# Attention and GEGLU block: a wait each for the two kinds of score products, a later tanh, and a rebuilt end

## The chip, the cores and the metric

The kernel runs on one core of a Trainium2 chip. The metric is device time in microseconds (us). The kernel before takes 1311.1 us, the median of three runs (1309.63 to 1311.43). A core has five engines that work beside each other, each with its own queue in order: TensorE (PE in the profile, with its weight loads listed as PEld), VectorE (DVE), ScalarE (ACT), GpSimd (POOL) and SyncE (SP), which here issues the transfers. They wait for each other through semaphores.

## What is computed

One transformer block on x of 1 x 2048 x 512 in bf16, cut to what matters:

```python
h  = x + A(layernorm(x))                 # 32 heads of 16
h2 = h + B(layernorm(h))                 # GEGLU, 512 -> 1792 -> 512
# A: q, k, v = split(xn @ wqkv); p = softmax(q @ k.T * 16**-0.5); (p @ v) @ wo
# B: (gelu_tanh(hn @ w_gate) * (hn @ w_up)) @ w_down
```

The softmax takes off the maximum of each row before the exponential, so the scores are made twice: once with queries on the partitions, to find the maximum, and once with keys on the partitions, to be exponentiated and multiplied with V.

## The kernel before

**Units and ticks.** The work is cut into 64 units: eight groups `gi` of 256 query rows, eight slots of four heads each. A unit has 16 ticks, and the main loop at the end of the kernel emits the work of all engines tick by tick. In a tick there are two streams. The first makes the maxima: `p1_pair` issues two matmuls of 32 x 512 (L665) into two banks of `pbank` (a bank is 128 x 512 in float32; there are eight), and `p1_consume` lets DVE reduce both banks with one maximum (L674). It has banks 0 to 3, two pairs in turn. The second stream runs `P2_START` = 24 ticks behind: `p2_tile` is called twice, each call two matmuls of 32 x 256 (L735) into one bank, and `p2_consume` lets ACT exponentiate each bank (L747) into one of 34 tiles named PTM, PTE and PTG. It takes its banks from a list of four (4 to 7), shared with the dense work. So the first stream alone runs in ticks 0 to 23, both in 24 to 1023, and the second alone in ticks 1024 to 1047, which is called the drain here.

**Maxima.** POOL joins the maxima in three steps (L685 to L692 and L700 to L708), a transfer transposes them, and POOL adds them into QT (L719).

**Dense work.** Everything else of TensorE is cut into pieces by Python generators and one piece (or a few, ahead of the second stream) is issued per tick by `dense.piece()`: the projections of q, k and v; `item_pv`, the product with V (L761, 16 matmuls a piece, four pieces a unit, with a fixed place in the unit); `item_ofin`, which transposes the result and normalises it (POOL: L796 takes the power -1 of 16 columns, L800 multiplies); `item_oproj`; and the feed-forward network, `item_gate` and `item_up` (L948) for seven pairs of columns f of each group, and `item_down` (L996). A piece states a cost of up to 3. Where a tick's piece costs under 2, `dummy` fills up with matmuls of 128 x 512 on ones (L1150), whose result nobody reads.

**GELU beside attention.** A gate tile is copied by ACT to `g_sb`. `gelu_chain` puts three operations into POOL's stream (L938, L939, L940), and when the last of them is emitted, `later` is deferred by one tick and then emits the tanh on ACT (L931); it waits further where ACT has other additional work in this tick or the one before (`act_extra`). One tick later `second` adds two more POOL operations (L936, L937), and a last one multiplies with the up tile into GUT (L989). There are two buffers for a chain, taken by f modulo 2; `item_gate` waits while its buffer is busy. `PoolStream` gives POOL a budget of 1.19 us a tick, from costs that are written in by hand, and issues in order.

**Waits.** `Plan.op` works out which semaphores an instruction must wait for. Between `group_begin` and `group_end` all waits of the instructions are taken together and put in front of the first one:

```python
            P.group_begin("pe")
            t1 = p1_pair(tick // 16, tick % 16, gp1) if p1_ok else []
            t2l = [p2_tile(t2 // 16, t2 % 16, 1 - gp1, 0)] if p2_ok else []
            P.group_end("pe")
```

So the pair for the maximum and the first of the two exponential tiles start when both DVE has left the pair's banks and ACT has left the tile's bank. The second tile has its own wait.

**The end.** After the drain, `tail_b` finishes the last group alone: the last slot's result is normalised (`tail_norm`, `tail_onT`), the last quarter of the output projection is added (L1108), the second layer norm is done for its two row tiles, the result is transposed (`tail_hnT`), and gate, up and down products of group 7 follow. `fill(n)` issues dense pieces that are left (the down products of group 6, L996, closed by the residual in L1000), or dummies, up to a cost of n. The norm before: for tile 1 ACT copies with a running sum (L1111) and squares with a running sum (L1113), and POOL works out mean, variance, power -0.5 and the normalised tile (`ln2_from_sums`, `ln2_finish`: L892 to L895, L910 to L913); for tile 0 DVE copies and takes statistics (L1115 to L1117), and POOL does the rest (`ln2_tail`, L902, and `ln2_finish` again), behind tile 1.

Of the kernel before, what the change touches and what calls it, by code (L numbers as in the profile page):

```python
# [209 lines left out]
ACT = mybir.ActivationFunctionType  # L210
ALU = mybir.AluOpType
# [5 lines left out]
EPS = 1e-5  # L217
# [5 lines left out]
ADDX = 4  # L223
LAGX = 8
PAUSE = 1


def bass_sequential_preLN__mha_block__geglu_ffn__prompt_kernel(nc, A_x, A_wqkv, A_wo, B_x, B_w_gate, B_w_up, B_w_down, out):
    dbg = None
    with ExitStack() as es:  # L230
# [236 lines left out]
        def defer(k, fn):  # L467
            deferred.append((dense.now + k, fn))
# [426 lines left out]
            o(lambda e: e.tensor_tensor(out=rstd2[:, tt_], in0=rstd2[:, tt_], in1=htmp[:, tt_], op=ALU.subtract), reads=[("rstd2", t), ("htmp", t)], writes=[("rstd2", t)])  # L895
            return ops + ln2_finish(gi, k, t)

        def ln2_tail(gi, k, t):
            tt_ = slice(t, t + 1)
            ops = []  # L900
            o = lambda fn, reads, writes, cost=0.2: ops.append((cost, lambda: P.op("pool", fn, reads=reads, writes=writes)))
            o(lambda e: e.tensor_scalar(out=rstd2[:, tt_], in0=mv2[:, t, 1:2], scalar1=EPS, scalar2=None, op0=ALU.add), reads=[("mv2", t)], writes=[("rstd2", t)])  # L902
            return ops + ln2_finish(gi, k, t)

        def ln2_finish(gi, k, t):
            hh = g_h(gi, k)
            tt_ = slice(t, t + 1)
# [13 lines left out]
        def gelu_chain(par, dE):  # L921

            th_ready[par] = False
            gs, ts_ = g_sb[:, par, :], th_sb[:, par, :]
            o = lambda cost, fn, reads, extra=(): (cost, lambda: P.op("pool", fn, reads=reads, writes=[("th", par)], extra_deps=extra))
            def later(n):
                if not force[0] and (dense.now in act_extra or (n < 3 and (dense.now - 1) in act_extra)):
                    defer(1, lambda: later(n + 1))
                    return
                act_extra.add(dense.now)  # L930
                P.op("act", lambda e: e.activation(out=ts_, in_=ts_, func=ACT.Tanh, scale=GC), reads=[("th", par)], writes=[("th", par)])  # L931
                defer(1, second)
            def second():
                def done():
                    th_ready[par] = True
                pool.add([o(0.62, lambda e: e.tensor_scalar(out=ts_, in0=ts_, scalar1=1.0, scalar2=0.5, op0=ALU.add, op1=ALU.mult), [("th", par)]),  # L936
                          o(1.27, lambda e: e.tensor_tensor(out=ts_, in0=ts_, in1=gs, op=ALU.mult), [("th", par), ("g", par)])], then=done)  # L937
            pool.add([o(1.04, lambda e: e.tensor_tensor(out=ts_, in0=gs, in1=gs, op=ALU.mult), [("g", par)], dE),  # L938
                      o(0.62, lambda e: e.tensor_scalar(out=ts_, in0=ts_, scalar1=0.044715, scalar2=1.0, op0=ALU.mult, op1=ALU.add), [("th", par)]),  # L939
                      o(1.27, lambda e: e.tensor_tensor(out=ts_, in0=ts_, in1=gs, op=ALU.mult), [("th", par), ("g", par)])], then=lambda: defer(1, lambda: later(0)))  # L940

        def gate_up_mms(b, gi, f, w, nm):
            hT = hnT_l[gi % 2]
# [154 lines left out]
        def tail_b():  # L1098
            P.op("act", lambda e: e.activation(out=htmp[:, 0:1], in_=nhalf[:, 0:1], func=ACT.Gelu_apprx_tanh), reads=["nhalf"], writes=[("htmp", 0)])
            fill(2)  # L1100
            while not a_done[0]:
                fill(1)
            in_bank(tail_norm)
            fill(2)
            in_bank(tail_onT)
            fill(2)
            for k in range(2):
                P.op("pe", lambda e, k=k: e.matmul(pbank[:, k, :], OnT[:, k, 3, :], wo_sb[:, 3, :], start=False, stop=True),  # L1108
                     reads=[("OHb", 0), "wo"], writes=[("pb", k)], sig=True)
            t0 = 2 * GL  # L1110
            P.op("act", lambda e: e.activation(out=g_h(GL, 1), in_=pbank[:, 1, :], func=ACT.Copy, accum_out=hsum[:, t0 + 1:t0 + 2]),  # L1111
                 reads=[("pb", 1)], writes=[("h", 1, 1), ("hsum", t0 + 1)])
            P.op("act", lambda e: e.activation(out=hn_sb[:, 1, :], in_=g_h(GL, 1), func=ACT.Square, accum_out=hsq[:, t0 + 1:t0 + 2]),  # L1113
                 reads=[("h", 1, 1)], writes=[("OH", 1), ("hsq", t0 + 1)])
            P.op("dve", lambda e: e.tensor_copy(out=g_h(GL, 0), in_=pbank[:, 0, :]), reads=[("pb", 0)], writes=[("h", 1, 0)])  # L1115
            P.op("dve", lambda e: e.bn_stats(out=stats2[:, t0, :], in_=g_h(GL, 0)), reads=[("h", 1, 0)], writes=[("stats2", t0)])
            P.op("dve", lambda e: e.bn_aggr(out=mv2[:, t0, :], in_=stats2[:, t0, :]), reads=[("stats2", t0)], writes=[("mv2", t0)])  # L1117
            pool.add(ln2_from_sums(GL, 1, t0 + 1))
            pool.add(ln2_tail(GL, 0, t0))
            fill(14)  # L1120
            for k in (1, 0):
                in_bank(tail_hnT, k)
            fill(2)
            while dense.busy():
                dense.pause = 0
                dense.piece()
                run_deferred(tick, flush=True)
            gb = [2, 3, 4, 5, 6, 7]
            NP = NFC // 2
            for f in range(NP + 2):  # L1130
                if f < NP:
                    for it, b in ((item_gate, gb[(2 * f) % 6]), (item_up, gb[(2 * f + 1) % 6])):
                        for _ in it(b, GL, f):
                            pass
                if f >= 2:
                    for fc in (2 * (f - 2), 2 * (f - 2) + 1):
                        for k in range(2):
                            down_mm(k, GL, k, fc)
            dG = rdeps("G", [("x", cc) for cc in range(NCH)])
            for k in range(2):  # L1140
                down_last(k, GL, k)
                if k == 0:
                    P.op("act", lambda e: e.activation(out=out_sb[:, 0, :], in_=pbank[:, 0, :], func=ACT.Copy), reads=[("pb", 0)], writes=[("osb", 0)], extra_deps=dG)
                else:
                    P.op("dve", lambda e: e.tensor_copy(out=out_sb[:, 1, :], in_=pbank[:, 1, :]), reads=[("pb", 1)], writes=[("osb", 1)], extra_deps=dG)
                P.dma("sp", lambda e, k=k: e.dma_start(out=outv[:, 2 * GL + k, :], in_=out_sb[:, k, :]), ("out", k), reads=[("osb", k)], writes=[("outd", 2 * GL + k)])

        def dummy(b, n):
            for i in range(n):
                P.op("pe", lambda e: e.matmul(pbank[:, b, :], ident[:], ones_bf[:, 0:512], start=True, stop=True),  # L1150
                     reads=["ident", "ones_bf"], writes=[("pb", b)], sig=False)
# [4 lines left out]
        while True:  # L1156
            p1_ok = tick < 16 * NU
            t2 = tick - P2_START
            p2_ok = (0 <= t2 < 16 * NU)
            if not p1_ok and not p2_ok:  # L1160
                break
            if tick == P2_START - 4:
                dense.single = True
                if dense.gen is not None:
                    banks.free.remove(dense.bank)
            if p2_ok and not p2_started:
                p2_started = True
            dve_free[0] = not p1_ok
            dense.tick(tick)
            gp1 = tick % 2  # L1170
            P.group_begin("pe")
            t1 = p1_pair(tick // 16, tick % 16, gp1) if p1_ok else []
            t2l = [p2_tile(t2 // 16, t2 % 16, 1 - gp1, 0)] if p2_ok else []
            P.group_end("pe")
            if p2_ok:
                t2l.append(p2_tile(t2 // 16, t2 % 16, 1 - gp1, 1))
            if t1:
                p1_consume(tick // 16, t1)
                if tick % 16 in (8, 12):
                    pool.spend(0.7)  # L1180
                    negm_part(tick // 16, 1 if tick % 16 == 8 else 2)
                if tick % 16 == 15:
                    pool.spend(1.8)
                    negm_pre(tick // 16)
                    negm_post(tick // 16)
            if t2l:
                p2_consume(t2 // 16, t2l)
            if p2_ok and t2 % 16 == 0:
                dense.add(item_pv, t2 // 16, front=True, est=5, not_before=tick + PV_T[0])
            cost = dense.piece()  # L1190
            if cost and not p2_started:
                dense.piece()
            if (cost or 0) < 2:
                dummy(banks.free[0], 2 - (cost or 0))
            run_deferred(tick)
            pool.tick()
            if w_pieces and tick % 16 in (7, 9, 11, 13):
                w_piece()
            tick += 1
# [39 lines left out]
```

## Time and profile before

| what | value |
|---|---|
| median of three runs | 1311.1 us (1309.63 to 1311.43) |
| the profiled execution | 1310.51 us, of which the span of instructions is 1308.4 us |
| mean granted clock of TensorE | 0.986 |
| PE, DVE, ACT, POOL busy | 1179.9, 1203.9, 1201.2, 763.6 us |
| 1024 reductions for the maximum (L674, DVE) | 1173.8 us, from 35.1 to 1236.2 us |
| 2048 exponentials (L747, ACT) | 735.5 + 226.1 + 135.8 us |
| fillers (L1150, PE) | 822, 258.2 us |
| tanh (L931, ACT) | 49, 30.9 us; ACT waited 11.4 us for them |
| DVE waiting for score products in front of a maximum | 39.4 us in all |
| drain and end, 1235 to 1308.4 us | 73.4 us; granted clock 0.66 and 0.91 in its two halves |

The page gives the busy time of each engine and then its groups of instructions: line, engine, operation, what is written and read, the count, the busy time and the mean time of one, and behind a bar the idle time of the engine just ahead of them with what ended most of it. A line of the timeline has the start, the length, engine, line, operation and, in brackets, the idle time ahead and its releaser. Busy times of ACT and DVE overlap a little from one instruction to the next: an exponential is listed at 643 ns, and four in a row take 1.96 us. A releaser is inferred: a wait that is put down to ACT may also have been the queue itself.

### The profile page before, as it was taken

Reading aid. Unit: us, or ns where it says so; the run is one execution under the profiler, and the core shown is the slowest. Engines: PE = TensorE matmul, PEld = TensorE weight load, DVE = VectorE, ACT = ScalarE, POOL = GpSimd, SP = SyncE. Lnnn points to the kernel's source line nnn. Section 1 sums busy time; section 2 is a strip of 40 time slices with the busy share of each in tenths; the row PEclk is TensorE's granted clock in tenths of the full one; section 3 lists DMA queues with packets and bytes.
Section 4 is the critical chain, followed back from the end, with each engine's and each line's share of the span. In section 5 each row is a group of like instructions: output and inputs, shape, how many; then the busy total and the mean of one; then the engine's idle time right before and its main releaser. Section 6 shows DMA issues by size and latency. Waiting matters only on the chain.

```text
span 1308.4 us, 31442 instructions
## 1 busy us (share of the span) xinstructions
PE 1179.9 (90%) x12678; PEld 408.4 (31%) x12678; DVE 1203.9 (92%) x1101; ACT 1201.2 (92%) x2440; POOL 763.6 (58%) x1534
## 2 busy tenths in 40 slices
PE   4999988999998999999999999999999999989998
PEld 2222222333223332233223332233323332233325
DVE  5899999999999999999999999999999999999702
ACT  3599999999999999999999999999999999999962
POOL 5567663477536773477635774467734775367721
PEclk9999999999999999999999999999999999999959
DMA  3110003200010000100011000100001000100000
GB/s 129 45 29 25 16 24 126 73 5 6 5 28 14 6 5 8 34 6 6 4 29 14 6 4 10 30 9 4 6 26 17 4 6 5 28 14 6 14 1 17
DMA packets 48689, 27.45 MB, mean 21 GB/s; under 512 B 34977, under 2 KB 47009, under 8 KB 48545
## 3 DMA queue, kind: packets, MB, share of 16 engines
q1 hardware_dynamic: 48544, 25.44, 7.4%
q8 instruction: 101, 1.65, 0.5%
q14 instruction: 44, 0.35, 0.1%
HBM read 11.80 MB, written 2.10 MB: 11 GB/s over the span
## 4 chain that ended last, share of the span: by engine, by line
ACT 29%; PE 29%; DVE 24%; POOL 14%; issue 3%; DMA 1%; POOLq 0%
DVE PM L674 23%; ACT PTM L747 15%; PE pbank L761 6%; ACT PTG L747 5%; PE pbank L665 5%; PE pbank L1150 5%; PE pbank L735 5%; POOL LINV L796 4%; PE pbank L996 4%; ACT PTE L747 3%; ACT th_sb L931 2%; POOL th_sb L940 2%; POOL th_sb L938 2%; PE pbank L615 1%; PE pbank L563 1%
## 5 line engine op out<-in xcount | busy, mean ns | idle before, releaser
L674 DVE TENSOR_REDUCE PM<-pbank 128x2 f32<-128x1024 f32 x1024 | 1173.8, 1217 | 39.4 <-PE pbank L735 21.0
L747 ACT ACTIVATE PTM<-pbank 128x512 bf16<-128x512 f32 x1388 | 735.5, 643 | 20.2 <-PE pbank L735 12.0
L735 PE MATMUL pbank<-QT,KT 32*128 32x256 bf16 x4096 | 490.3, 275 | 19.2 <-ACT PTM L747 10.0
L665 PE MATMUL pbank<-KT,QT 32*128 32x512 bf16 x2048 | 398.4, 385 | 12.0 <-DVE PM L674 5.4
L1150 PE MATMUL pbank<-ones_bf,ident 128*128 128x512 bf16 x822 | 258.2, 390 | 37.2 <-ACT u_sb L528 8.3
L747 ACT ACTIVATE PTG<-pbank 128x512 bf16<-128x512 f32 x420 | 226.1, 632 | 5.0 <-PE pbank L735 3.4
L665 PEld LDWEIGHTS pbank<-KT,QT 32*128 32x128 bf16 x2048 | 99.0, 91 | 352.6 <-DVE PM L674 148.8
L735 PEld LDWEIGHTS pbank<-QT,KT 32*128 32x128 bf16 x4096 | 160.9, 92 | 72.0 <-ACT PTM L747 34.9
L761 PE MATMUL pbank<-PTM,VA 128*17 128x256 bf16 x2776 | 157.1, 279 | 14.8 <-PE pbank L761 0.2
L747 ACT ACTIVATE PTE<-pbank 128x512 bf16<-128x512 f32 x240 | 135.8, 643 | 3.8 <-PE pbank L735 2.2
L700 POOL TENSOR_TENSOR MX<-PM,MX 128x8 f32<-128x8 f32 x64 | 12.9, 202 | 168.2 <-DVE PM L674 168.2
L796 POOL TENSOR_TENSOR LINV<-OAT,negone 128x16 f32<-128x16 f32 (+1 forms) x32 | 92.7, 2898 | 12.8 <-DVE OAT L517 12.8
L1150 PEld LDWEIGHTS pbank<-ones_bf,ident 128*128 128x128 bf16 x822 | 49.6, 97 | 146.1 <-ACT PTM L747 88.7
L689 POOL TENSOR_TENSOR MX<-PM,MX 128x8 f32<-128x8 f32 x64 | 13.0, 203 | 119.2 <-DVE PM L674 119.2
L761 PEld LDWEIGHTS pbank<-PTM,VA 128*17 128x17 bf16 x2776 | 42.7, 87 | 108.9 <-PE pbank L761 77.0
L948 PE MATMUL pbank<-hnT_l,wg_sb 128*128 128x256 bf16 x448 | 67.9, 277 | 4.2 <-ACT PTG L747 0.6
L948 PE MATMUL pbank<-hnT_l,wu_sb 128*128 128x256 bf16 x448 | 67.4, 276 | 3.2 <-ACT PTG L747 0.2
L996 PE MATMUL pbank<-wd_sb,GUT 128*128 128x512 bf16 x224 | 61.5, 386 | 3.6
L940 POOL TENSOR_TENSOR th_sb<-th_sb,g_sb 128x512 f32<-128x512 f32 x49 | 62.2, 1269 | 4.1
L937 POOL TENSOR_TENSOR th_sb<-th_sb,g_sb 128x512 f32<-128x512 f32 x49 | 62.1, 1267 | 2.9
L989 POOL TENSOR_TENSOR GUT<-th_sb,u_sb 128x512 bf16<-128x512 f32 x49 | 62.2, 1269 | 2.7
L719 POOL TENSOR_TENSOR QT<-QT,STG 128x256 bf16<-128x256 bf16 x64 | 42.8, 669 | 33.9 <-DMA STG<-ST 33.9
(128 smaller groups left out, 1074.6 us busy)
## 6 DMA issues: line engine op xcount, KB each, us to landing
QKS<-QKS SPq DMA_DIRECT2D x32, 112.0 KB, 2.1
x_sb<-in_A_x_dram SPq DMA_DIRECT2D x4, 512.0 KB, 5.4
xres<-in_A_x_dram SPq DMA_DIRECT2D x16, 128.0 KB, 2.2
out_dram<-out_sb SPq DMA_DIRECT2D x16, 128.0 KB, 1.7
wg_sb<-in_B_w_gate_dram SPq DMA_DIRECT2D x4, 448.0 KB, 4.8
wu_sb<-in_B_w_up_dram SPq DMA_DIRECT2D x4, 448.0 KB, 4.8
wqkv_sb<-in_A_wqkv_dram SPq DMA_DIRECT2D x1, 1536.0 KB, 10.2
wd_sb<-in_B_w_down_dram SPq DMA_DIRECT2D x3, 512.0 KB, 5.9
```

What stands on the lines that cost most here:

```text
L665: P.op("pe", lambda e, g=g, b=b: e.matmul(pbank[:, b, :], QT[32 * g:32 * g + 32, c, slot, 128 * qt:128 * qt + 128], KT[32 * g:32 * g + 32, ...
L674: P.op("dve", lambda e: e.tensor_reduce(out=PM[:, par, qt, kc, g:g + 2], in_=pbank[:, b:b + 2, :], axis=AX.X, op=ALU.max), reads=[("pb", b ...
L735: P.op("pe", lambda e, kt=kt, i=i: e.matmul(pbank[:, b, 256 * i:256 * i + 256], KT[32 * g:32 * g + 32, slot, 128 * kt:128 * kt + 128], QT[ ...
L747: P.op("act", lambda e, b=b, pi=pi: e.activation(out=PTt(pi), in_=pbank[:, b, :], func=ACT.Exp), reads=[("pb", b)], writes=[("PT", pi)], e ...
L761: P.op("pe", lambda e, g=g, kt=kt, pi=pi, i=i: e.matmul(pbank[32 * g:32 * g + 17, b, 0:256], VA[:, kt, 4 * slot + g, :], PTt(pi)[:, 256 * ...
L796: P.op("pool", lambda e: e.tensor_tensor(out=li, in0=oat4[:, :, :, 16], in1=negone[:, 0:8 * ns].rearrange("p (q h) -> p q h", q=2), op=ALU ...
L937: o(1.27, lambda e: e.tensor_tensor(out=ts_, in0=ts_, in1=gs, op=ALU.mult), [("th", par), ("g", par)])], then=done)
L940: o(1.27, lambda e: e.tensor_tensor(out=ts_, in0=ts_, in1=gs, op=ALU.mult), [("th", par), ("g", par)])], then=lambda: defer(1, lambda: lat ...
L948: P.op("pe", lambda e, dc=dc, fc=fc, i=i: e.matmul(pbank[:, b, 256 * i:256 * i + 256], w[:, dc, 128 * fc:128 * fc + 128], hT[:, dc, :], st ...
L989: P.op("pool", lambda e: e.tensor_tensor(out=o_ap, in0=shp(ts_), in1=shp(us), op=ALU.mult), reads=[("th", par), ("u", par)], writes=o_keys ...
L996: P.op("pe", lambda e: e.matmul(pbank[:, b, :], GUT[:, fc, 128 * k:128 * k + 128], wd_sb[:, fc, :], start=(fc == 0), stop=False), reads=[( ...
L1150: P.op("pe", lambda e: e.matmul(pbank[:, b, :], ident[:], ones_bf[:, 0:512], start=True, stop=True), reads=["ident", "ones_bf"], writes=[( ...
```

## The change

Four edits. The group around the score products is taken away, so each instruction has its own wait. The tanh is deferred by two ticks in place of one. In the drain a tick is filled up to a cost of 3 in place of 2. The second layer norm of the end is written anew: statistics for both tiles on DVE, copies on ACT, two POOL operations for both tiles together, normalising on DVE; the filler behind it has cost 18 in place of 14, and the tiles are transposed in the order 0, 1.

```diff
+TANH_LAG = 2
...
-                      ...], then=lambda: defer(1, lambda: later(0)))
+                      ...], then=lambda: defer(TANH_LAG, lambda: later(0)))
...
             t0 = 2 * GL
-            P.op("act", ... activation(out=g_h(GL, 1), in_=pbank[:, 1, :], func=ACT.Copy, accum_out=hsum[...]))
-            P.op("act", ... activation(out=hn_sb[:, 1, :], in_=g_h(GL, 1), func=ACT.Square, accum_out=hsq[...]))
-            P.op("dve", ... tensor_copy(out=g_h(GL, 0), in_=pbank[:, 0, :]))
-            P.op("dve", ... bn_stats(out=stats2[:, t0, :], in_=g_h(GL, 0)))
-            P.op("dve", ... bn_aggr(out=mv2[:, t0, :], in_=stats2[:, t0, :]))
-            pool.add(ln2_from_sums(GL, 1, t0 + 1))
-            pool.add(ln2_tail(GL, 0, t0))
-            fill(14)
-            for k in (1, 0):
+            tok = P.op("dve", ... bn_stats(out=stats2[:, t0, :], in_=pbank[:, 0, :]))
+            P.op("act", ... activation(out=g_h(GL, 1), in_=pbank[:, 1, :], func=ACT.Copy))
+            P.op("act", ... activation(out=g_h(GL, 0), in_=pbank[:, 0, :], func=ACT.Copy), extra_deps=[tok])
+            P.op("dve", ... bn_stats(out=stats2[:, t0 + 1, :], in_=g_h(GL, 1)))
+            for k in range(2):
+                P.op("dve", ... bn_aggr(out=mv2[:, t0 + k, :], in_=stats2[:, t0 + k, :]))
+            tt = slice(t0, t0 + 2)
+            P.op("pool", ... tensor_scalar(out=rstd2[:, tt], in0=mv2[:, tt, 1], scalar1=EPS, op0=ALU.add))
+            P.op("pool", ... tensor_tensor(out=rstd2[:, tt], in0=rstd2[:, tt], in1=nhalf[:, 0:2], op=ALU.pow))
+            for k in range(2):
+                P.op("dve", ... tensor_scalar(out=hn_sb[:, k, :], in0=g_h(GL, k), scalar1=mv2[:, t0 + k, 0:1], scalar2=rstd2[:, t0 + k:t0 + k + 1], op0=ALU.subtract, op1=ALU.mult))
+            fill(18)
+            for k in (0, 1):
                 in_bank(tail_hnT, k)
...
-            P.group_begin("pe")
             t1 = p1_pair(tick // 16, tick % 16, gp1) if p1_ok else []
             t2l = [p2_tile(t2 // 16, t2 % 16, 1 - gp1, 0)] if p2_ok else []
-            P.group_end("pe")
...
-            if (cost or 0) < 2:
-                dummy(banks.free[0], 2 - (cost or 0))
+            want = 2 if p1_ok else 3
+            if (cost or 0) < want:
+                dummy(banks.free[0], want - (cost or 0))
```

`ln2_tail` is removed with its only call.

More of the change, by code (lines that the diff above doesn't have):

```diff
@@ L896, in ln2_from_sums @@
             return ops + ln2_finish(gi, k, t)
[L898 to L903, printed above, removed]
         def ln2_finish(gi, k, t):
@@ L939, in gelu_chain @@
                       o(0.62, lambda e: e.tensor_scalar(out=ts_, in0=ts_, scalar1=0.044715, scalar2=1.0, op0=ALU.mult, op1=ALU.add), [("th", par)]),
-                      o(1.27, lambda e: e.tensor_tensor(out=ts_, in0=ts_, in1=gs, op=ALU.mult), [("th", par), ("g", par)])], then=lambda: defer(1, lambda: later(0)))
+                      o(1.27, lambda e: e.tensor_tensor(out=ts_, in0=ts_, in1=gs, op=ALU.mult), [("th", par), ("g", par)])], then=lambda: defer(TANH_LAG, lambda: later(0)))
         def gate_up_mms(b, gi, f, w, nm):
@@ L1110, in tail_b @@
             t0 = 2 * GL
[L1111 to L1115, printed above, removed]
@@ L1116, in tail_b @@
-            P.op("dve", lambda e: e.bn_stats(out=stats2[:, t0, :], in_=g_h(GL, 0)), reads=[("h", 1, 0)], writes=[("stats2", t0)])
-            P.op("dve", lambda e: e.bn_aggr(out=mv2[:, t0, :], in_=stats2[:, t0, :]), reads=[("stats2", t0)], writes=[("mv2", t0)])
-            pool.add(ln2_from_sums(GL, 1, t0 + 1))
-            pool.add(ln2_tail(GL, 0, t0))
-            fill(14)
-            for k in (1, 0):
+            tok = P.op("dve", lambda e: e.bn_stats(out=stats2[:, t0, :], in_=pbank[:, 0, :]), reads=[("pb", 0)], writes=[("stats2", t0)])
@@ new lines, in tail_b @@
+            P.op("act", lambda e: e.activation(out=g_h(GL, 1), in_=pbank[:, 1, :], func=ACT.Copy), reads=[("pb", 1)], writes=[("h", 1, 1)])
+            P.op("act", lambda e: e.activation(out=g_h(GL, 0), in_=pbank[:, 0, :], func=ACT.Copy), reads=[("pb", 0)], writes=[("h", 1, 0)], extra_deps=[tok])
+            P.op("dve", lambda e: e.bn_stats(out=stats2[:, t0 + 1, :], in_=g_h(GL, 1)), reads=[("h", 1, 1)], writes=[("stats2", t0 + 1)])
+            for k in range(2):
+                P.op("dve", lambda e, k=k: e.bn_aggr(out=mv2[:, t0 + k, :], in_=stats2[:, t0 + k, :]), reads=[("stats2", t0 + k)], writes=[("mv2", t0 + k)])
@@ new lines, in tail_b @@
+            both = lambda nm: [(nm, t0), (nm, t0 + 1)]
+            tt = slice(t0, t0 + 2)
+            P.op("pool", lambda e: e.tensor_scalar(out=rstd2[:, tt], in0=mv2[:, tt, 1], scalar1=EPS, scalar2=None, op0=ALU.add), reads=both("mv2"), writes=both("rstd2"))
+            P.op("pool", lambda e: e.tensor_tensor(out=rstd2[:, tt], in0=rstd2[:, tt], in1=nhalf[:, 0:2], op=ALU.pow), reads=both("rstd2") + ["nhalf"], writes=both("rstd2"))
+            for k in range(2):
+                P.op("dve", lambda e, k=k: e.tensor_scalar(out=hn_sb[:, k, :], in0=g_h(GL, k), scalar1=mv2[:, t0 + k, 0:1], scalar2=rstd2[:, t0 + k:t0 + k + 1], op0=ALU.subtract, op1=ALU.mult),
+                     reads=[("h", 1, k), ("mv2", t0 + k), ("rstd2", t0 + k)], writes=[("OH", k)])
```

## The prediction, made before the result was known

> **What bounds the kernel.** I read the page's busy times and slices first, then its groups, the chain of waits, and the timeline at the places where the two busiest engines stop together.
>
> ```profile
> PE 1179.9 (90%) x12678; PEld 408.4 (31%) x12678; DVE 1203.9 (92%) x1101; ACT 1201.2 (92%) x2440; POOL 763.6 (58%) x1534
> PEclk9999999999999999999999999999999999999959
> ...
> L674 DVE TENSOR_REDUCE PM<-pbank 128x2 f32<-128x1024 f32 x1024 | 1173.8, 1217 | 39.4 <-PE pbank L735 21.0
> L747 ACT ACTIVATE PTM<-pbank 128x512 bf16<-128x512 f32 x1388 | 735.5, 643 | 20.2 <-PE pbank L735 12.0
> ```
>
> DVE and ACT are tied at 92%. The 1024 reductions start 1.131 us apart where nothing disturbs them (from the starts of the L674 rows), and two exponentials take 0.98 us of ACT ("4 in 1.96" in the chain), so a tick has only 0.15 us of room for ACT's other work. The next to last slice shows the clock of TensorE at 5. Three places lose time.
>
> (1) Steady phase, 75 to 1235 us: the stop of one engine passes to the other.
>
> ```profile
> 1019.54 0.60 PE L1150 MATMUL pbank<-ones_bf,ident 128*128 128x512 bf16 x2
> ...
> 1019.81 0.63 ACT L931 ACTIVATE th_sb<-th_sb 128x512 f32<-128x512 f32 x1 [0.32 <-POOL th_sb L940]
> 1020.07 0.09 PEld L665 LDWEIGHTS pbank<-KT,QT 32*128 32x128 bf16 x2 [0.42 <-DVE PM L674]
> ...
> 1020.98 0.11 PEld L735 LDWEIGHTS pbank<-QT,KT 32*128 32x128 bf16 x2 [0.79 <-ACT PTM L747]
> ...
> 1022.09 0.09 PEld L665 LDWEIGHTS pbank<-KT,QT 32*128 32x128 bf16 x2 [0.22 <-ACT PTM L747]
> ...
> 1022.53 2.35 DVE L674 TENSOR_REDUCE PM<-pbank 128x2 f32<-128x1024 f32 x2 [0.68 <-PE pbank L735]
> ```
>
> Follow it down: the tanh (L931) reaches ACT before POOL has made its input; ACT stands 0.32 us; the exponentials behind it are late, so the second tile's matmuls (L735) wait for a bank; 16 products with V (L761) are behind those in PE's queue; the next pair for the maximum (L665) is late; DVE idles 0.68 us. Waits of this kind total 10.2 us over 20 tanhs before 1235 us; DVE's losses of 0.77 to 1.85 us at the same 20 places sum to 18.5 us.
>
> (2) The drain, 1235 to 1270.6, and (3) the end.
>
> ```profile
> 1243.22:1246.63 3.41, 1.96 (x24) 0.47 (x24) 0.00 (x0) 2.19 (x5) 2.49 (x4) 1.00 0.00 0
> 1246.63:1250.05 3.42, 3.28 (x30) 0.96 (x30) 0.42 (x1) 2.44 (x6) 2.76 (x3) 0.50 0.02 5
> ...
> 1280.77:1284.18 3.41, 1.37 (x12) 0.78 (x13) 0.42 (x1) 0.60 (x1) 1.95 (x5) 1.00 0.00 0
> 1284.18:1287.59 3.41, 3.41 (x15) 2.10 (x14) 0.69 (x1) 0.52 (x1) 0.00 (x0) 0.50 0.11 38
> ```
>
> Columns: length, then busy time of PE, PEld, DVE, ACT, POOL, then the granted clock. At 1244.3 the last tanh waits 1.21 us, PE idles 1.40 us, and the next stretch gets half the clock, which lasts until 1273.94. A filler tick takes 0.86 us before (1238.66, 1239.52, 1240.38) and 1.51 us after the drop (1262.25, 1263.76). The norm at the end idles PE again, with the same effect on the first gate matmuls.
>
> **The change, part by part.**
>
> *Separate waits.* In a tick PE issues the pair for the maximum (L665) and the first exponential tile (L735). Removed is ACT's wait in front of the pair; it now stands in front of the tile. Queued behind it are the second tile, the dense piece or filler and the next pair; DVE waits for that pair. So the pair can gain at most what it waited for ACT: 94.2 us over 314 ticks stand before it under the three exponential tiles. But 0.21 to 0.22 us of such a row after L761 and L948, and 0.42 after fillers, also stand where nothing was waited for ("issue"). After L761, 235 of 248 pairs start at this least gap. Of the DVE stops after 75 us, 24.3 us, not one has a pair that ACT released in the 0.06 us before its start: PE's queue, held earlier by the second tile, sets them. Direct gain taken: 0; bounds 0 and 5 us. If the cover (waits already fulfilled) goes, the cost is below, in rival E.
>
> *TANH_LAG 2.* The tanh is emitted one tick later, behind two more exponentials (0.98 us). The longest of the 20 waits is 1.04 us, the usual ones 0.32 and 0.81, so they go almost wholly: 10.2 us of ACT. ACT has no idle between such a stall and the DVE stop, so I count it one for one: **-10.2 us**. Ends: -18.5 (every DVE stop there goes), and +3: the tanh moves from two ticks to one tick ahead of the evacuation of OA. A tanh without any wait (1226.58) already costs DVE 0.33 us there; 20 times that plus the 14 tanhs that now cost nothing (0.33 each) is 11.2 us against 10.2 saved, and I allow 2 more for GELU chains that come a tick later. I take ACT's own stall, the nearest row. Each chain holds its buffer one tick longer; the 822 fillers in PE's queue show that dense work has room.
>
> *Three fillers per drain tick.* With the last tanh a tick later, ACT reaches it about 1 us later, POOL's product is due at 1245.50, and I expect the clock to stay at 1. A third filler costs 0.22 us at full clock (0.60 for two, 0.38 for one) and 0.40 at half (1.03 and 0.63). Ticks 1024 to 1033 took 13.38 us (1235.06 to 1248.44). After: two with up-projection at 1.15 + 0.22, four with filler at 0.86 + 0.22, four with products at 1.18 (mean of 1.13, 1.30, 1.12) + 0.22: 12.7. Ticks 1034 to 1047 took 22.16; after: eleven at 1.08, three at 1.40: 16.1. PE then sets the pace; ACT needs 1.03. Sum **-6.8**; without the third filler it would be 5 us more. What is late next is PE itself.
>
> *The end.* From 1270.6 to L1108 only the clock changes: the last products and OA's copy -0.8 (1.43 us at half clock, then only the last exponentials are waited for), three down matmuls and two transposes from OA's copy at 1272.10 to the reciprocal at 1274.22 -1.0. Then the norm. Before, counted from 1276.34 (first down matmul behind L1108): two ACT passes, POOL's chain of 1.3 us of scalars and 0.77 normalising per tile, both tiles in a row on one engine, transposes at 1283.13, the second group of down matmuls in front of the gate: L948 at 1285.12, that is +8.78. After: DVE statistics 0.69, ACT copies 0.60 (the second waits for the statistics of bank 0, done 0.1 us earlier), statistics 0.69, two aggregations 0.18, POOL add 0.25 and power. A power on two columns is not in the trace; one column takes 0.58, four take 1.05: 0.74. DVE normalising 0.40 + 0.32 (L361: 1.27 for four). Result at +3.9. In front of the transposes PE has 18 matmuls of filler work (17 down, one residual; nine took 2.10): +4.1, so filler sets it. Transposes, copies 0.42 and 0.60: L948 at +5.5: -3.3. No window is then idle enough for the half clock: the first 16 gate and up matmuls 1.75 instead of 2.96 us, -1.2. Sum **-6.3** (ends -3.5 and -7.5). DVE's evacuation to out_sb queues behind the normalising, 2 us later; its store is hidden behind 20 us of gate and up matmuls. No DMA is moved past another on SP.
>
> **Sum.** 10.2 + 6.8 + 6.3 = 23.3 us from 1310.51 (the profiled execution; span 1308.4 and 2.1 around it) gives 1287.2. The median of the runs is 0.6 above that execution: 1288 us.
>
> **Rivals.**
> A, the forecast: 1288 (own range 1281 to 1295), chance 0.48.
> B, the tanh only changes its place: DVE stops in front of OA's copy stay as large. For it: the 0.33 us at a tanh that waited for nothing. Against: 0.77 where it waited. -13.1: 1298; 0.22.
> D, every DVE stop at the 20 places goes: -18.5 - 13.1: 1279.5; 0.10.
> C, the clock falls in the drain all the same, and three fillers are paid at half clock: first ten ticks +0.9, fourteen ticks +0.42 each, +5.9; the end saves 4.5: 1310.5 - 10.2 + 0.9 + 5.9 - 4.5 = 1302.6, say 1303; 0.08. Against it: the stretches of 3.41 us ahead of the four drops have PE busy 2.27 (342.10), 2.26 (942.85), 1.96 (1243.22) and 1.37 (1280.77), among the lowest of the trace. For it: two others as low, 2.14 (454.74) and 2.26 (792.66), had no drop, so PE's busy time is not all of the cause. The Trainium skill, in "TensorE: Matmul & The Clock Gate", Part 1 and the closing table, lets the gate close only after about a whole window (3.4 us) without matmuls; by that rule a stop of 1.40 us is not the cause, removing it need not keep the clock, and C would be the outcome. The trace speaks for the shorter stop: the drop begins 0.1 us before the stop ends, and no other stop of PE is near.
> E, slower: the pair and the first tile no longer start together. Before, two L665 and two to four L735 run within 0.39 us (1020.07, 1020.09). If each split costs one more pass, 0.21 us, and PE is the bound where 16 products fill the tick (1.12 to 1.30 us against 1.131), four ticks in 16 of 64 units pay: 256 x 0.21 = 54 us, 1310.5 + 54 - 23.3 = 1341. It decides from about 110 such ticks. Against it: after L761 both waits have ended when PE arrives, and matmuls with fulfilled waits start within 0.02 us of each other. 0.07. [...]
> F, nothing measurable, by parts of B, C and E together: 0.05.
>
> **The numbers.** Faster: A, B, C, D, 0.88; slower: E, 0.07; within 0.2% (about what a measurement of this kernel can tell from no change): 0.05. The range leaves out C and E and F, 0.20: 1278 to 1302.
>
> **What would show it.** Right: waits of L931 for L940 under 2 us in all; DVE stops for L735 from 21 to about 10 us; granted clock 1.00 from 1235 to the end; drain ticks of 1.08 us; L948 5.5 us behind L1108. Wrong: half clock in the drain (C), DVE stops unchanged in front of OA's copy (B), pairs and tiles 0.2 us apart after L761 (E).

## The result and the profile after

The changed kernel takes 1385.01 us (median of four runs, 1384.64 to 1385.15) beside 1311.26 us of the kernel before: ratio 1.0563, 95% interval 1.0544 to 1.0581. The forecast was 1288 us, faster, with a range of 1278 to 1302. It was wrong in sign and by 97 us. The profiled execution has a span of 1382.6 us.

The page of the changed kernel, the lines that answer to those of before (line numbers have shifted: L674 has become L675, L735 L736, L665 L666, L747 L748, L1150 L1148, L931 L925, L761 L762, L948 L942):

```profile
PE 1274.5 (92%) x12702; PEld 425.9 (31%) x12702; DVE 1242.4 (90%) x1104; ACT 1235.8 (89%) x2438; POOL 761.1 (55%) x1523
...
PEclk9999999999999999999999999999999999999999
...
L675 DVE TENSOR_REDUCE PM<-pbank 128x2 f32<-128x1024 f32 x1024 | 1211.5, 1221 | 87.0 <-PE pbank L736 37.7
L748 ACT ACTIVATE PTM<-pbank 128x512 bf16<-128x512 f32 x1388 | 757.7, 619 | 61.8 <-PE pbank L736 50.7
...
L736 PEld LDWEIGHTS pbank<-QT,KT 32*128 32x128 bf16 x4096 | 144.1, 92 | 190.8 <-PE pbank L666 154.9
```

DVE and ACT are both less busy as a share; the idle time before a maximum has gone from 39.4 to 87.0 us, and the exponentials in PTM wait 61.8 us where they waited 20.2. The clock is 9 in every slice: that part of the forecast came out. The last line is the new one. In front of the weight loads of the exponential tiles stand 190.8 us, and 154.9 of them are put down to the pair for the maximum, an instruction of TensorE itself. Before, the same line had 72.0 us, most of it for ACT:

```profile
L735 PEld LDWEIGHTS pbank<-QT,KT 32*128 32x128 bf16 x4096 | 160.9, 92 | 72.0 <-ACT PTM L747 34.9 <-ACT PTG L747 11.0 <-ACT PTE L747 9.1
```

The list of waits of the changed kernel counts them (total, times, longest):

```profile
PEld pbank L666 <- issue: 302.3, 947, 0.4
...
PEld pbank L736 <- PE pbank L666: 154.9, 432, 0.4
```

The kernel before has no such entry. The timeline of the weight loads shows where it stands. First the kernel before, two ticks with a filler ahead of them:

```profile
1229.21 0.11 PEld L1150 LDWEIGHTS pbank<-ones_bf,ident 128*128 128x128 bf16 x2 [0.23 <-ACT PTM L747]
1229.75 0.09 PEld L665 LDWEIGHTS pbank<-KT,QT 32*128 32x128 bf16 x2 [0.42 <-issue]
1229.75 0.12 PEld L735 LDWEIGHTS pbank<-QT,KT 32*128 32x128 bf16 x4
1230.08 0.11 PEld L1150 LDWEIGHTS pbank<-ones_bf,ident 128*128 128x128 bf16 x2 [0.21 <-ACT PTM L747]
1230.62 0.09 PEld L665 LDWEIGHTS pbank<-KT,QT 32*128 32x128 bf16 x2 [0.42 <-DVE PM L674]
1230.62 0.12 PEld L735 LDWEIGHTS pbank<-QT,KT 32*128 32x128 bf16 x4
```

Then the changed kernel, one tick with products with V ahead of it and two with fillers:

```profile
1313.29 0.11 PEld L762 LDWEIGHTS pbank<-PTM,VA 128*17 128x17 bf16 x8 [0.36 <-PE pbank L762]
1313.62 0.09 PEld L666 LDWEIGHTS pbank<-KT,QT 32*128 32x128 bf16 x2 [0.22 <-issue]
1313.63 0.12 PEld L736 LDWEIGHTS pbank<-QT,KT 32*128 32x128 bf16 x4
1314.13 0.11 PEld L1148 LDWEIGHTS pbank<-ones_bf,ident 128*128 128x128 bf16 x2 [0.38 <-ACT PTM L748]
1314.67 0.09 PEld L666 LDWEIGHTS pbank<-KT,QT 32*128 32x128 bf16 x2 [0.42 <-issue]
1315.12 0.12 PEld L736 LDWEIGHTS pbank<-QT,KT 32*128 32x128 bf16 x4 [0.36 <-PE pbank L666]
1315.44 0.11 PEld L1148 LDWEIGHTS pbank<-ones_bf,ident 128*128 128x128 bf16 x2 [0.21 <-ACT PTM L748]
1315.98 0.10 PEld L666 LDWEIGHTS pbank<-KT,QT 32*128 32x128 bf16 x2 [0.42 <-issue]
```

Before, pair and tile load 0.01 us apart and a filler tick takes 0.87 us. After, behind the products with V they still load together (1313.62 and 1313.63), but behind fillers the tile comes 0.45 us after its pair (1314.67 and 1315.12), and the tick takes 1.31 us, more than the 1.131 us of a reduction. In the whole trace this holds for all 432 ticks behind a filler and for no other kind.

**Where the wait comes from** can be read in the planner. A filler does not signal (`sig=False`), so `op` marks its bank as written at "TensorE's next signal" (the last branch of `op`, L107). That next signal is the second matmul of the next pair. The first tile then takes the filler's bank, the first of the list, finds that mark and must wait for it. Such a wait is left out only as long as that signal has not been counted (`_waits_for`, L75); when the tile is planned the pair has been, so it becomes a real wait of TensorE for itself. `group_end` dropped it, because it leaves out every wait on its own engine whose signal lies in the group:

```python
            if k == eng and v > e.group_count:
                continue
```

So the group did two things: it joined the waits, and it removed one, of TensorE for itself, that served nothing: the filler's product is read by no one, and the kernel before ran without this wait.

**What it costs.** From one pair's start to the next, the 432 ticks behind a filler take 1.397 us on average in the changed kernel and 1.128 in the version with the group put back (first experiment): 432 x 0.269 = 116 us more. The 248 ticks behind products with V become shorter, 1.172 to 1.089: 21 us less. There is less to wait for there, since DVE has caught up (the pairs' weight loads wait 32.2 us for it in the changed kernel and 135.9 with the group). The difference, 95 us, is what the last reduction starts later (1320.46 and 1226.05: 94.4 us).

### The profile page after: what moved, and what is told of

Read it like the earlier page. It is cut to its first block, busy times and chain, and to the rows that moved or that the text cites. A ratio compares the mean times of both kernels' runs of the same rounds, so it can differ in the third digit from the quotient of the medians.

```text
span 1382.6 us, 30975 instructions
## 1 busy us (share of the span) xinstructions
PE 1274.5 (92%) x12702; PEld 425.9 (31%) x12702; DVE 1242.4 (90%) x1104; ACT 1235.8 (89%) x2438; POOL 761.1 (55%) x1523
## 4 chain that ended last, share of the span: by engine, by line
PE 65%; ACT 28%; issue 3%; DVE 2%; POOL 1%; DMA 0%
ACT PTM L748 16%; PE pbank L1148 15%; PE pbank L736 15%; PE pbank L666 14%; PE pbank L762 10%; ACT PTG L748 6%; PE pbank L990 4%; ACT PTE L748 2%; PE pbank L788 2%; ACT th_sb L925 1%; DVE PM L675 1%; ACT g_sb L529 1%; PE pbank L616 1%; PE pbank L564 1%; ACT u_sb L529 1%
## 5 line engine op out<-in xcount | busy, mean ns | idle before, releaser
L675 DVE TENSOR_REDUCE PM<-pbank 128x2 f32<-128x1024 f32 x1024 | 1211.5, 1221 | 87.0 <-PE pbank L736 37.7
L748 ACT ACTIVATE PTM<-pbank 128x512 bf16<-128x512 f32 x1388 | 757.7, 619 | 61.8 <-PE pbank L736 50.7
L736 PE MATMUL pbank<-QT,KT 32*128 32x256 bf16 x4096 | 454.2, 273 | 30.6
L666 PE MATMUL pbank<-KT,QT 32*128 32x512 bf16 x2048 | 397.3, 385 | 0.8 <-ACT QT L591 0.8
L1148 PE MATMUL pbank<-ones_bf,ident 128*128 128x512 bf16 x846 | 261.2, 384 | 22.6 <-ACT u_sb L529 8.3
L748 ACT ACTIVATE PTG<-pbank 128x512 bf16<-128x512 f32 x420 | 230.8, 614 | 14.2 <-PE pbank L736 11.0
L736 PEld LDWEIGHTS pbank<-QT,KT 32*128 32x128 bf16 x4096 | 144.1, 92 | 190.8 <-PE pbank L666 154.9
L666 PEld LDWEIGHTS pbank<-KT,QT 32*128 32x128 bf16 x2048 | 96.2, 90 | 335.8 <-issue 302.3
L762 PE MATMUL pbank<-PTM,VA 128*17 128x256 bf16 x2776 | 154.9, 275 | 13.4 <-PE pbank L762 0.2
L748 ACT ACTIVATE PTE<-pbank 128x512 bf16<-128x512 f32 x240 | 137.6, 611 | 10.1 <-PE pbank L736 7.8
L1148 PEld LDWEIGHTS pbank<-ones_bf,ident 128*128 128x128 bf16 x846 | 51.6, 97 | 117.7 <-ACT PTM L748 55.5
L762 PEld LDWEIGHTS pbank<-PTM,VA 128*17 128x17 bf16 x2776 | 42.6, 87 | 103.5 <-PE pbank L762 83.4
L942 PE MATMUL pbank<-hnT_l,wu_sb 128*128 128x256 bf16 x448 | 67.1, 275 | 5.1 <-ACT PTG L748 0.2
L942 PE MATMUL pbank<-hnT_l,wg_sb 128*128 128x256 bf16 x448 | 67.1, 275 | 1.6
L931 POOL TENSOR_TENSOR th_sb<-th_sb,g_sb 128x512 f32<-128x512 f32 x49 | 62.0, 1266 | 2.9
```

Source lines behind the costliest of these rows:

```text
L666: P.op("pe", lambda e, g=g, b=b: e.matmul(pbank[:, b, :], QT[32 * g:32 * g + 32, c, slot, 128 * qt:128 * qt + 128], KT[32 * g:32 * g + 32, ...
L675: P.op("dve", lambda e: e.tensor_reduce(out=PM[:, par, qt, kc, g:g + 2], in_=pbank[:, b:b + 2, :], axis=AX.X, op=ALU.max), reads=[("pb", b ...
L736: P.op("pe", lambda e, kt=kt, i=i: e.matmul(pbank[:, b, 256 * i:256 * i + 256], KT[32 * g:32 * g + 32, slot, 128 * kt:128 * kt + 128], QT[ ...
L748: P.op("act", lambda e, b=b, pi=pi: e.activation(out=PTt(pi), in_=pbank[:, b, :], func=ACT.Exp), reads=[("pb", b)], writes=[("PT", pi)], e ...
L762: P.op("pe", lambda e, g=g, kt=kt, pi=pi, i=i: e.matmul(pbank[32 * g:32 * g + 17, b, 0:256], VA[:, kt, 4 * slot + g, :], PTt(pi)[:, 256 * ...
L942: P.op("pe", lambda e, dc=dc, fc=fc, i=i: e.matmul(pbank[:, b, 256 * i:256 * i + 256], w[:, dc, 128 * fc:128 * fc + 128], hT[:, dc, :], st ...
```

## The experiments

**The group put back.** The changed kernel with its three other edits.

```diff
+            P.group_begin("pe")
             t1 = p1_pair(tick // 16, tick % 16, gp1) if p1_ok else []
             t2l = [p2_tile(t2 // 16, t2 % 16, 1 - gp1, 0)] if p2_ok else []
+            P.group_end("pe")
```

> The changed kernel with only the group around the score products put back. Theory S (self-wait): in the changed kernel a tile that takes the bank of a filler waits for TensorE's own pair of matmuls, because a filler does not signal and its mark is the next signal of TensorE, the pair's; the group drops such waits on the engine itself. It puts down to this the 154.9 us in front of L736 (432 times 0.36) and expects about 1289 us here (1310.5 less the 10 to 12 us that the drain and end gained, less up to 10 for the tanh), no wait of L736 for L666, and a first tile within 0.02 us of its pair. Theory P (split pack): the loss comes from starting pair and tile apart; it expects the same 1289 here and cannot be told from S by this run. Theory T (tanh): the loss comes from the later tanh, after which GpSimd waits 16.3 us for ScalarE; it expects over 1360.

Measured: 1289.75 us (1289.13 to 1290.95), ratio to the kernel before 0.9835 (0.9820 to 0.9849). No wait of L736 for L666 is left. The whole loss goes with this edit, and theory T falls: GpSimd still waits 12.4 us for the tanh here, and yet the kernel is 22 us faster than the one before.

**Only the group taken away**, from the kernel before (the two lines of the diff above, removed).

> The kernel before with only the group taken away. Theories S and P: about 1311 + 85 = 1396 us (the last reduction started 85.5 us later in the changed kernel), perhaps less where ScalarE's waits already covered some of it, 1380 to 1400; about 430 waits of the tile for the pair of 0.36 us each. Theory T: about 1311.

Measured: 1392.77 us (1385.20 to 1394.73), ratio 1.0608 (1.0577 to 1.0640), with

```profile
PEld pbank L735 <- PE pbank L665: 155.0, 432, 0.4
```

The same 155 us as in the changed kernel. The edit alone makes the loss. The other three then take only 8 us of it away (1392.77 to 1385.01), where they bring 22 with the group in place: ACT's waits for the tanh are down to 0.7 us in this version, from 11.4 before, so a later tanh has next to nothing left to save. The trace of this version is of the slowest of its four executions; in its drain the clock is at half for 27.3 us, behind a stop of TensorE of 0.85 us at the last tanh.

**A wait each, but no mark by the filler.** This tells a wait of TensorE for itself (S) from the loss of the joint start (P): pair and tile keep separate waits.

```diff
-                     reads=["ident", "ones_bf"], writes=[("pb", b)], sig=False)
+                     reads=["ident", "ones_bf"], writes=[], sig=False, extra_deps=P._deps([], [("pb", b)]))
```

> The changed kernel, pair and tile with a wait each, but a filler keeps its own waits and is no longer noted as the writer of its bank, so the tile behind it has no wait on TensorE itself (TensorE works in order, and the kernel before had no such wait either). Theory S: as with the group put back, about 1289 us, within 5 us of it; a tile 0.01 us behind its pair. Theory P: still about 1385, since the waits of pair and tile stay apart.

Measured: 1289.28 us (1288.81 to 1289.61), ratio 0.9831 (0.9814 to 0.9847), and behind fillers the weight loads stand together again:

```profile
1219.46 0.11 PEld L1148 LDWEIGHTS pbank<-ones_bf,ident 128*128 128x128 bf16 x2 [0.38 <-ACT PTM L748]
1220.00 0.09 PEld L666 LDWEIGHTS pbank<-KT,QT 32*128 32x128 bf16 x2 [0.42 <-issue]
1220.01 0.12 PEld L736 LDWEIGHTS pbank<-QT,KT 32*128 32x128 bf16 x4
```

P falls. With the mark gone, a wait each is as good as the joint one: the pair stands free of ACT, and that is worth nothing that can be measured (1289.28 beside 1289.75).

**The filler signals.** The mark is then the filler's own end and not the pair's, a smaller dose of the same wait.

```diff
-                     reads=["ident", "ones_bf"], writes=[("pb", b)], sig=False)
+                     reads=["ident", "ones_bf"], writes=[("pb", b)], sig=(i == n - 1))
```

> The changed kernel, but the last filler of a tick signals, so that the tile behind it waits for the filler and not for the pair. Theory S: the wait shrinks with the distance: two fillers end 0.60 us after the start of the first, the pair starts 0.54 us after it, so the tile starts about 0.1 us behind the pair in place of 0.45; time between the version without the wait and the changed kernel, near the first: 1290 to 1310. Theory P: still about 1385.

Measured: 1298.40 us (1297.13 to 1299.23), ratio 0.9899 (0.9884 to 0.9913).

```profile
1227.41 0.11 PEld L1148 LDWEIGHTS pbank<-ones_bf,ident 128*128 128x128 bf16 x2 [0.21 <-issue]
1227.95 0.09 PEld L666 LDWEIGHTS pbank<-KT,QT 32*128 32x128 bf16 x2 [0.42 <-issue]
1228.08 0.12 PEld L736 LDWEIGHTS pbank<-QT,KT 32*128 32x128 bf16 x4
```

The tile follows its pair by 0.13 us (expected 0.1) in place of 0.45, and the time lies 9 us above the version without the wait and 87 below the changed kernel. Of the 9 us, 7.0 lie ahead of the last reduction's start (1231.93 and 1224.97) and 2.2 in the drain (31.2 and 29.0). S stands: a shorter wait brings a smaller loss, though not in proportion.

**The three other edits, one at a time**, each on the kernel before: `TANH_LAG` alone, the end alone, the third filler alone, by the lines of the diff above.

> The kernel before with the tanh deferred by two ticks and nothing else. The prediction's term: 10.2 us from the tanh, and besides no half clock in the drain (no stop of TensorE at the last tanh), which at two fillers a tick is worth 6.8 plus about 5 us, and about 1.8 us of the end up to L1108: 1312 - 10 - 12 - 2 = 1288 us. Rival B (the tanh only changes its place): 1298. If the clock falls in the drain all the same: about 1302.

> The kernel before with only the end rebuilt. The prediction's term: 3.3 us of shorter norm and 1.2 us of half clock behind it: 1312 - 4.5 = 1307.5 us; half clock in the drain as before.

> The kernel before with only three fillers a drain tick. The last tanh still stops TensorE for about 1.4 us, so the clock still falls. If it stays at half for the rest of the drain, as before: 14 ticks with 0.40 more each and ten with 0.2: about 8 us slower, 1320. If the third filler brings the full clock back after a stretch of 3.41 us or two: ticks of 1.08 in place of 1.51, 4 to 6 us faster, 1306 to 1308.

Measured: the tanh 1290.07 us (1288.54 to 1290.22), ratio 0.9841 (0.9823 to 0.9858); the end 1305.07 (1304.42 to 1307.85), ratio 0.9962 (0.9949 to 0.9976); the third filler 1304.32 (1300.00 to 1306.68), ratio 0.9948 (0.9930 to 0.9967). The first two came near what was expected: 20.0 us faster than the kernel before (24 expected) and 5.0 (4.5 expected). The traces of the kernel before and of the later tanh differ by 20.4 us: 9.6 us ahead of the last reduction, 9.0 us of drain (34.3 to 25.4) and 1.8 us from there to the output projection, where the clock is now full. With the end alone the last tanh still stops TensorE, 1.38 us, and the clock is at half for the same 27.3 us. The third fits neither branch. In its trace the clock never fell in the drain (1.00 over all of 1234.56 to 1263.36): ACT comes to the last tanh later, the wait of 1.21 us is 0.07, and TensorE has no stop. That is the same cure as the later tanh, by another way, but it is shown for this execution alone, the fastest of six (1300.00 us, granted clock 0.999). The other five have clocks of 0.991 to 0.996, so some of them may have lost the clock in the drain; there is no trace of them.

**Two fillers with the later tanh and the new end** (the group put back, `want = 2`).

> The changed kernel with the group put back and two fillers a drain tick, as before (tanh and end stay changed). If the stop at the last tanh alone caused the half clock: full clock all through, and about 5 us less than with three fillers, 1285 us. If two fillers are too few to hold the clock: half clock in the drain, about 1297 us.

Measured: 1285.38 us (1284.75 to 1285.71), ratio 0.9806 (0.9790 to 0.9823). The drain, by the stretches from the last reduction's end to the last exponential's end. First three fillers (group put back), then two:

```profile
1227.27:1256.28 29.01, 27.26 (x270) 9.08 (x276) 1.97 (x4) 26.32 (x50) 13.69 (x18) 1.00 0.05 13
```

```profile
1226.55:1251.91 25.36, 24.16 (x255) 7.94 (x252) 1.98 (x4) 24.92 (x50) 13.69 (x18) 1.00 0.05 15
```

The clock (third column from the right) is 1.00 in both: once the tanh is out of the way, two fillers hold it, and the third only takes TensorE's time, 3.65 us here.

**The last variants.** A wait each without the mark, with two fillers; the group with one filler in the drain; and no mark with one filler in every tick.

> Pair and tile with a wait each, the filler not noted as writer of its bank, later tanh, new end, two fillers a drain tick. If a wait each is worth nothing in itself (1289.28 beside 1289.75 with three fillers): 1285 us, as the version with the group and two fillers. If it is worth something: below 1284.

> Group put back, later tanh, new end, one filler a drain tick. Three fillers took 29.0 us for the drain and two 25.4. If ScalarE sets the pace at two already (about 1.0 us a tick), the same 1285 us, as long as the clock holds; if TensorE still does, about 1282; if one filler is too few for the clock: 1290 or more.

> As the version with two fillers and no mark, but one filler in every tick, the steady phase too. The reductions set the pace there, so fewer fillers can save at most the 14 us that VectorE still stands idle for TensorE; if the clock falls anywhere for long, ticks of 1.5 us: over 1300 us. If neither: 1283 to 1285.

Measured: 1285.14 us (1285.05 to 1285.38), ratio 0.9805 (0.9790 to 0.9821); 1293.33 (1291.39 to 1293.45), ratio 0.9868 (0.9850 to 0.9886); 1305.11 (1302.44 to 1306.74), ratio 0.9955 (0.9940 to 0.9970). One filler is too few: in the drain the clock is at half for 20.5 us from 1239.9 on, and with one in every tick it is at half for some 100 us in eleven stretches. The best versions, 1285.1 and 1285.4 us, cannot be told apart; both are about 25 us faster than the kernel before and 100 us faster than the changed one.

## Why the prediction was wrong, step by step

**Separate waits: wrong.** The step said "direct gain taken: 0; bounds 0 and 5 us" and looked only at the waits for ACT and DVE. It measured 81 us of loss on the kernel before and 95 beside the three other edits. What failed is the reading of the edit: "Removed is ACT's wait in front of the pair; it now stands in front of the tile". That is all it was taken to do, while the joining of waits had also removed TensorE's wait for itself. In its place the runs showed 432 such waits of 0.36 us, 154.9 us in all. No row of the trace of before could show that wait, because it was not there; the code could, in three places that stand in the listing (the filler's `sig=False`, the mark of an instruction without signal, and the condition in `group_end`). For a wait that the trace of before does not show, the price was in the trace all the same: a pair's matmuls take 0.385 us, 432 ticks follow a filler, and 432 x 0.385 is 166 us before anything hides it.

**Rival E: right in its effect, wrong in place and size.** It named pair and tile drifting apart, put this behind the products with V, and priced it at 0.21 us for 256 ticks. There the two stay together. They part behind fillers, by 0.45 us, 432 times. Its argument against itself, that fulfilled waits start within 0.02 us, was true; the wait in question was a new one that is never fulfilled when TensorE arrives. Giving up the joint wait was not the cause either: without the mark, separate waits leave pair and tile 0.01 us apart.

**TANH_LAG: right for the kernel with the group, but it could not be added to the first edit.** ACT's waits for the tanh are gone altogether, and the last reduction starts 9.6 us earlier with this edit alone (1225.35 in place of 1234.96); the forecast was 10.2. With the group put back, DVE's stops for the tiles fall from 21.0 to 10.8 us, where about 10 were forecast. B and D are both off by more than 8 us. In the changed kernel these 9.6 us are not to be had: the first edit alone leaves 0.7 us of the waits for the tanh, and the last reduction starts at 1318.15 with it and at 1320.46 with the later tanh besides. The sum took its terms to be independent, and this one was not.

**The drain: right in its cause, the term a little too large.** The clock stays at 1.00. With three fillers the drain takes 29.0 us and not 34.3, 5.3 less where 6.8 were forecast; a filler tick takes 1.08 us as worked out (two of them in the changed kernel run 1324.91, 1325.99, 1327.07). C falls. In every trace with a stop of TensorE at the last tanh (1.40 us before, 1.38 with the end alone, 0.85 with the group alone taken away) the clock dropped for 27.3 us, and with the stop gone, by the later tanh or by the third filler, it did not. The rule of the Trainium skill that stood with C ("TensorE: Matmul & The Clock Gate", Part 1, about a whole window without matmuls) does not hold here: a stop of less than half of 3.41 us was enough. The prediction also put the third filler at about 5 us of cost once the clock holds; it measured 4.4 in the time of the whole kernel (1289.75 and 1285.38).

**The end: right.** In the changed kernel (first column start, second length):

```profile
1354.79 0.59 PE L1102 MATMUL pbank<-wo_sb,OnT 128*128 128x512 bf16 x2
...
1357.37 0.71 POOL L1114 TENSOR_TENSOR rstd<-rstd,nhalf 128x2 f32<-128x2 f32 x1
1358.20 0.73 DVE L1116 TENSOR_SCALAR OnT<-xres,mv,rstd 128x512 bf16<-128x512 bf16 x2 [1.24 <-POOL rstd L1114]
...
1358.91 0.65 PEld L1078 LDWEIGHTS pbank<-ident,OnT 128*128 128x128 bf16 x8
...
1360.51 1.03 PE L942 MATMUL pbank<-hnT_l,wg_sb 128*128 128x256 bf16 x8
```

The power on two columns takes 0.71 us (0.74 worked out); from the end of the output projection to the first gate matmul 5.13 us in place of 8.63, 3.5 less (3.3 worked out); from there to the end of the span 22.04 in place of 23.27, 1.2 less (1.2 worked out); from the last exponential to the output projection's end 4.4 in place of 6.0, 1.6 less (0.8 + 1.0 worked out). The term was 6.3, and it came to 6.3.

Without the first edit the sum of 23.3 us would have been nearly right: 1289.75 beside 1312.17 is 22.4. One term of the sum, the one set at zero, decided the sign.

## What to carry to other kernels

When an edit takes a grouping of waits apart, work out for every instruction in it what it would wait for alone, its own engine's semaphore included: an instruction without a signal hands its mark to the next one that signals, and whoever reuses its buffer then waits for a later instruction than the one it depends on. A filler's result is read by no one, so let it wait for its buffer and leave no mark; a signal of its own is second best (9 us slower here). Fillers that hold the clock are worth their time only up to the number that holds it (here two a tick in the drain: one lets the clock fall, a third costs 4 us). Terms worked out on the kernel before can be added only as long as no edit takes away the wait that another one saves.

## What the runs showed that was not expected

A stop of TensorE of 1.40 us was followed by 27.3 us at half clock, in which the clock did not come back though TensorE was busy 21.78 of the 22.16 us from 1248.44 to 1270.60; why it stays away so long is open. In the drain, two fillers a tick held the clock in all three traces without such a stop, and one filler lost it for 20.5 us. The power on GpSimd takes 0.58, 0.71, 1.05, 1.65 and 2.93 us on 1, 2, 4, 8 and 16 columns (on four, the first of four took 2.46). That the wait of an engine for itself was the largest loss of this kernel, 155 us of idle queue, was the main surprise; 0.45 us lay between two instructions of one queue that had started 0.01 us apart.
